# Attention and MLP on one core: loads queued earlier, pair 0 on hardware queues, two more pairs turned by transposing transfers

## The chip, the cores and the metric

One core of a Trainium2 chip. The metric is the device time of one execution in microseconds, median over several runs; lower is better. Engines are named as in the profile: PE (TensorE), PEld (its weight loads), DVE (VectorE), ACT (ScalarE), POOL (GpSimd), SP (SyncE). A "pair" is two of the twelve heads of one batch entry; there are 48 pairs. "Turning" q, k or x is transposing it for PE, either by matmuls against an identity on PE, or by a transposing transfer on SP's hardware queue.

## The reference

```python
# q, k, v: (8, 12, 448, 64) float32; w_in: (768, 2048); w_out: (2048, 768)
scores = (q @ k.transpose(0, 1, 3, 2)) / np.sqrt(64)
attn = np.exp(scores - scores.max(-1, keepdims=True))
attn = attn / (attn.sum(-1, keepdims=True) + 1e-09)
x = (attn @ v).transpose(0, 2, 1, 3).reshape(3584, 768)
h = x @ w_in
out = np.maximum(0.01 * h, h) @ w_out          # (3584, 768) float32
```

## The kernel before

Pairs 0 to 5 (batch entry 0) open the kernel: scores on PE, exponentials on ACT, weighted values on PE. From pair 6 on, "clusters" of attention work are woven between the matmuls of the MLP over the batch entry before. Loads of the first 18 pairs and of all weights go through POOL's software queue, which casts to bf16 on the way; they stand in POOL's program between casts that POOL does itself.

```python
def load_soft(u, n, which):            # n pairs of q, k or v in one transfer (POOL's queue)
    ...
def supply(u):                         # POOL's work in opening pair u
    if u == 0:
        cast(0, (2,), fast); cast(2, (0, 1), fast); cast(1, (2,), fast)   # fast: on DVE
        cast(3); cast(2, (2,))                                            # on POOL
        load(6)
        return
    load_w({1: 1}.get(u, 0))           # one of eight weight slices
    cast(u + 3)
    load({3: 8, 5: 10}.get(u, NU))     # two pairs
    load_w({2: 1, 4: 1, 5: 1}.get(u, 0))

def cluster(g):                        # t, r = divmod(g, 4); u = 3 * t
    if turn_q < NPE:                   # NPE = 14: pairs below it are turned on PE
        transposes(turn_q)
    ...                                # scores, exponentials, values
    if r < 3:
        cast(u + 3 + r)
        load(u + 5 + r)
        load_w({9: 1, 10: 1, 13: 1}.get(g, 0))   # the last three w_out slices
    if r > 0:
        dma_transposes(u + 2 + r)      # from pair NPE on: transposing transfer on SP

def mlp(i):
    ...                                # h = leaky(x @ w_in), 16 groups, then per output half w:
    for m in range(MD):                # MD = 16; m >= 8 with w = 1 reads the LAST w_out slice
        nc.tensor.matmul(ps[:, :NW], h[:, m, ts(c, P)], w_out_sb[:, m, ts(w, NW)], ...)
```

The softmax here doesn't subtract the row's maximum and nothing guards it: scores larger than these inputs give would overflow.

## Time and profile before

| | before |
|---|---|
| time, median | 421.32 us (421.07 to 422.21) |
| span in the profile | 418.9 us, granted clock 0.996 |
| PE busy | 407.3 us |
| first matmuls of the MLP start | 27.92 us |
| last w_out slice issued, landed | 59.41, 72.8 us |

PE is busy for 97% of the span, so time can be won only where PE waits, where it is slowed, or where it is given less work. The lines and their reading are in the prediction.

### The profile page before, as it was taken

The numbers are of one execution on the slowest core, as the hardware profiler recorded it, in microseconds if no ns is written. First come the engines' busy times: TensorE is split into PE (matmuls) and PEld (weight loads), VectorE is DVE, ScalarE is ACT, GpSimd is POOL, SyncE is SP. The second block draws the span as 40 slices with busy tenths as digits, with TensorE's granted clock in tenths as the row PEclk, the third lists the DMA queues.
The fourth block names the chain that finished last, engine by engine and source line by source line (L and its number), as shares of the span: only waits on it lengthen the run. The fifth ranks groups of instructions, "written<-read, shape, count | busy, mean of one in ns | idle before, by whom it ended". The sixth has DMA issues, their size and how long they took to land.

```text
span 418.9 us, 8949 instructions
## 1 busy us (share of the span) xinstructions
PE 407.3 (97%) x3730; PEld 235.4 (56%) x3744; DVE 104.0 (25%) x293; ACT 228.0 (54%) x321; POOL 107.3 (26%) x179
## 2 busy tenths in 40 slices
PE   7899999999999999999999999999999999999995
PEld 2565665554555566554556656554465666654562
DVE  3653342311223113220132212221022211310021
ACT  4897882467442784466724584467643587214200
POOL 8865765321111313120311212131130200000000
PEclk9899999999999999999999999999999999999999
DMA  8999999982666848585465847768264541130032
GB/s 103 191 203 174 160 195 159 192 217 71 161 162 174 180 113 196 140 210 119 110 160 155 214 112 176 196 150 187 77 170 127 127 49 24 50 88 0 0 77 76
DMA packets 96249, 57.00 MB, mean 136 GB/s; under 512 B 53200, under 2 KB 92624, under 8 KB 96208
## 3 DMA queue, kind: packets, MB, share of 16 engines
q1 hardware_dynamic: 76352, 43.94, 44.2%
q0 software_dynamic: 19856, 12.49, 22.0%
q8 instruction: 29, 0.48, 0.5%
q14 instruction: 12, 0.10, 0.1%
HBM read 45.61 MB, written 11.01 MB: 135 GB/s over the span
## 4 chain that ended last, share of the span: by engine, by line
PE 81%; DMA 12%; POOL 4%; issue 1%; DVE 0%; POOLq 0%
PE mm L330 33%; PE mm L301 31%; PE pv L245 10%; PE sc L224 8%; DMA fv<-in_v_dram 7%; DMA w_out_sb<-in_moe_w_out_dram 3%; DMA fk<-in_k_dram 2%; POOL fq L102 1%; POOL fk L102 1%; POOL v L137 1%; POOL qkb L135 0%; DVE o L334 0%; POOL fv L102 0%; PE tr L209 0%; POOL ident masks.py:199 0%
## 5 line engine op out<-in xcount | busy, mean ns | idle before, releaser
L233 ACT ACTIVATE e<-sc 112x896 bf16<-112x896 f32 x192 | 165.0, 915 | 105.4 <-PE sc L224 105.0
L330 PE MATMUL mm<-w_out_sb,h 128*128 128x384 bf16 x896 | 150.4, 326 | 0.6 <-DVE x L253 0.2
L301 PE MATMUL mm<-xT,w_in_sb 128*128 128x384 bf16 (+1 forms) x742 | 147.8, 352 | 0.9 <-DVE x L253 0.2
L330 PEld LDWEIGHTS <-h 128*128 128x128 bf16 x896 | 85.9, 98 | 55.7 <-issue 0.8
L301 PEld LDWEIGHTS <-w_in_sb 128*128 128x128 bf16 x768 | 72.9, 98 | 66.2 <-issue 1.2
L316 ACT ACTIVATE h<-mm 128x512 bf16<-128x512 f32 (+1 forms) x126 | 68.7, 546 | 58.6 <-PE mm L301 57.4
L245 PEld LDWEIGHTS <-e 112*128 112x128 bf16 x1536 | 56.9, 98 | 26.2 <-issue 16.5
L137 POOL CAST v<-fv 112x512 bf16<-112x512 f32 x30 | 18.6, 618 | 193.2 <-PE pv L245 189.3
L245 PE MATMUL pv<-v,e 112*128 112x65 bf16 x1536 | 65.4, 195 | 0.4 <-DVE v L137 0.4
L334 DVE COPY o<-mm 128x384 f32<-128x384 f32 x56 | 31.2, 558 | 134.0 <-PE mm L330 134.0
L252 DVE RECIPROCAL rec<-pv 112x4 f32<-112x4 f32 x96 | 17.5, 182 | 150.4 <-PE pv L245 149.8
L224 PE MATMUL sc<-qkT 64*128 64x448 bf16 x384 | 49.6, 357 | 0.9 <-DVE qkT L213 0.7
L253 DVE TENSOR_TENSOR x<-pv,rec 112x256 bf16<-112x256 f32 x96 | 40.8, 425 | 3.3
L224 PEld LDWEIGHTS <-qkT 64*128 64x128 bf16 x384 | 13.6, 94 | 18.4 <-issue 9.2
L135 POOL CAST qkb<-fq 112x512 bf16<-112x512 f32 x30 | 18.5, 616 | 2.5 <-POOL v L137 1.3
L135 POOL CAST qkb<-fk 112x512 bf16<-112x512 f32 x30 | 18.5, 616 | 0.5 <-DMA fk<-in_k_dram 0.3
L135 POOL COPY qkb<-fq 112x512 bf16<-112x512 bf16 x15 | 9.4, 626 | 15.2 <-DMA fq<-in_q_dram 14.5
L137 POOL COPY v<-fv 112x512 bf16<-112x512 bf16 x16 | 9.8, 618 | 9.5 <-DMA fv<-in_v_dram 5.8
L213 DVE COPY qkT<-tr 128x896 bf16<-128x896 bf16 (+1 forms) x15 | 8.8, 589 | 11.7 <-PE tr L209 11.7
L209 PE MATMUL tr<-ident,qkb 112*128 112x112 bf16 x112 | 8.8, 220 | 1.5 <-DVE qkb L135 1.3
L135 POOL COPY qkb<-fk 112x512 bf16<-112x512 bf16 x15 | 9.4, 626 | 2.2 <-DMA fk<-in_k_dram 1.9
L209 PEld LDWEIGHTS <-qkb 112*128 112x128 bf16 x112 | 7.0, 101 | 4.2 <-DVE qkb L135 2.7
(26 smaller groups left out, 51.9 us busy)
## 6 DMA issues: line engine op xcount, KB each, us to landing
fq<-in_q_dram SPq DMA_DIRECT2D x30, 224.0 KB, 3.2
fk<-in_k_dram SPq DMA_DIRECT2D x30, 224.0 KB, 3.3
fv<-in_v_dram SPq DMA_DIRECT2D x30, 224.0 KB, 3.8
w_in_sb<-in_moe_w_in_dram POOLq DMA_DIRECT2D x4, 768.0 KB, 11.9
w_out_sb<-in_moe_w_out_dram POOLq DMA_DIRECT2D x4, 768.0 KB, 10.9
out_dram<-o SPq DMA_DIRECT2D x8, 336.0 KB, 3.5
out_dram<-o SPq DMA_DIRECT2D x8, 288.0 KB, 2.7
fv<-in_v_dram POOLq DMA_DIRECT2D x9, 224.0 KB, 8.1
```

The lines of the kernel that those rows point to most:

```text
L135: by(qk_sb[u][:, x].rearrange("p so h d -> p h so d"), f)
L137: by(v_sb[u % NV][:, :, :, :D], f)
L209: nc.tensor.transpose(tr[:, i, ts(so, SC)], qk_sb[u][:, i, so], ident[:SC, :SC])
L224: nc.tensor.matmul(ps[:, j, :S], t[j * D:(j + 1) * D, S + c * SC:S + c * SC + P], t[j * D:(j + 1) * D, :S], start=True, stop=True,)
L233: nc.scalar.activation(e[:, :, c, :], sc_t.pop((u, c))[:SC, :, :S], AX.Exp, scale=scale)
L245: nc.tensor.matmul(ps[:, qc, :], e[:, at:at + P], vt[:, j, c, :], start=(c == 0), stop=(c == NSC - 1),)
L252: nc.vector.reciprocal(rec, ps[:SC, :, D:])
L253: nc.vector.tensor_mul(x_t[u][:, :, j, :], ps[:SC, :, :D], rec.to_broadcast([SC, NSC, D]))
L301: nc.tensor.matmul(open_t[m][:, :n], w_in_sb[:, kk, ts(m, P)], xT[:, kk, at:at + n], start=(fresh and kk == kks[0]), stop=(kk == KD - 1),)
L316: nc.scalar.activation(h[:, m, :n], open_t.pop(m)[:, :n], AX.Prelu, alpha=0.01)
L330: nc.tensor.matmul(ps[:, :NW], h[:, m, ts(c, P)], w_out_sb[:, m, ts(w, NW)], start=(m == 0), stop=(m == MD - 1),)
L334: nc.vector.tensor_copy(o[c][:, ts(w, NW)], ps[:, :NW])
```

## The change

The intent: loads enter the software queue earlier, so that POOL never blocks the next load with a cast whose data is still coming; pair 0 arrives sooner by hardware queues; ACT has three chunks of pair 0 in hand before PE turns pair 1; and PE is relieved of turning pairs 12 and 13. The core of it, cuts marked:

```diff
-    load_soft(0, 1, (0, 1))
+    load_one(0, 1, nc.sync)            # k of pair 0 on SP's queue
+    load_soft(0, 1, (0,))
 ...
     load_soft(1, 1, (0, 1))
-    load_soft(0, 2, (2,))
-    load(2)
-    load(4)
+    load_soft(2, 2, (0, 1))            # q, k of pairs 2, 3
+    load_soft(1, 2, (2,))              # v of pairs 1, 2
+    load_soft(4, 2, (0, 1))
+    load_soft(3, 2, (2,))
+    load_soft(5, 1, (2,))
     load_w(1)
 ...
+    nc.scalar.copy(gate[:, :1], gate[:, 1:])
+    load_one(0, 2, nc.scalar)          # v of pair 0 on ACT's queue
 ...
-    cast(0, (0, 1), fast)
+    cast(0, (1,), lambda o, i: (nc.scalar.copy(o[:, 0], i[:, 0]), fast(o[:, 1], i[:, 1])))
+    cast(0, (0,), fast)
+    cast(0, (2,), nc.scalar.copy)
 ...
-    NPE = 14
+    NPE = 12
 ...
+        for what, n in {0: [('qk', 2), ('v', 1), ('v', 2), ('load', 6)],
+                        1: [('qk', 3), ('qk', 4), ('v', 3), ('w', 1)],
+                        2: [('qk', 5), ('v', 4), ('v', 5), ('load', 8)], ...   # supply(u)
 ...
-            warm_up(4)
+            warm_up(2)
         expo(u, 1)
+        if u == 0:
+            scores(u, 2)               # ahead of transposes(1)
```

More of the change, by code (lines that the diff above doesn't have):

```diff
@@ L108, in load_soft, with load_one, load @@
                 raw.setdefault(u + i, {})[x] = half(t, i)
-    def load(u, queues=(nc.sync,) * 3):
+    def load_one(u, x, queue):
+        b, hp = divmod(u, HP)
+        t = ld_pool.tile([SC, 2, NSC, D], F32, name="f" + "qkv"[x])
+        queue.dma_start(
+            out=t.rearrange("p h so d -> p h (so d)"),
+            in_=(q, k, v)[x][b, 2 * hp:2 * hp + 2].rearrange("h (p so) d -> p h (so d)", so=NSC),
+        )
+        raw.setdefault(u, {})[x] = t
+    def load(u):
         if u >= NU:
@@ L116, in load @@
             return
-        b, hp = divmod(u, HP)
-        raw[u] = {}
-        for a, name, eng in zip((q, k, v), ("fq", "fk", "fv"), queues):
-            t = ld_pool.tile([SC, 2, NSC, D], F32, name=name)
-            eng.dma_start(
-                out=t.rearrange("p h so d -> p h (so d)"),
-                in_=a[b, 2 * hp:2 * hp + 2].rearrange("h (p so) d -> p h (so d)", so=NSC),
-            )
-            raw[u][len(raw[u])] = t
+        for x in range(3):
+            load_one(u, x, nc.sync)
     def cast(u, parts=(0, 1, 2), by=nc.gpsimd.tensor_copy):
@@ L131, in cast @@
             f = raw[u].pop(x)
-            if x == 0:
+            if u not in qk_sb:
                 qk_sb[u] = cast_pool.tile([SC, 2, NSC, 2, D], BF16, name="qkb")
@@ L162 @@
     nc.vector.memset(warm, 0.0)
+    gate = const_pool.tile([P, 2], F32)
+    nc.vector.memset(gate, 0.0)
+    nc.scalar.copy(gate[:, :1], gate[:, 1:])
+    load_one(0, 2, nc.scalar)
     def warm_up(n):
@@ L204, in transposes @@
             return
-        for parts in ((0,), (1,)) if u == 0 else ((0, 1),):
+        for parts in ((1,), (0,)) if u == 0 else ((0, 1),):
             tr = turn_tile(bank)
@@ L340, in supply @@
     def supply(u):
-        if u == 0:
-            cast(0, (2,), fast)
-            cast(2, (0, 1), fast)
-            cast(1, (2,), fast)
-            cast(3)
-            cast(2, (2,))
-            load(6)
-            return
-        load_w({1: 1}.get(u, 0))
-        cast(u + 3)
-        load({3: 8, 5: 10}.get(u, NU))
-        load_w({2: 1, 4: 1, 5: 1}.get(u, 0))
+        for what, n in {0: [('qk', 2), ('v', 1), ('v', 2), ('load', 6)], 1: [('qk', 3), ('qk', 4), ('v', 3), ('w', 1)], 2: [('qk', 5), ('v', 4), ('v', 5), ('load', 8)], 3: [('qk', 6), ('v', 6), ('w', 1)], 4: [('qk', 7), ('v', 7), ('w', 1)], 5: [('qk', 8), ('v', 8), ('load', 10), ('w', 1)]}[u]:
+            if what == "qk":
+                cast(n, (0, 1), fast if n in (2, 3) else nc.gpsimd.tensor_copy)
+            elif what == "v":
+                cast(n, (2,))
+            elif what == "load":
+                load(n)
+            else:
+                load_w(n)
     def first(u):
@@ L369, in first @@
             supply(u)
-        scores(u, 2)
+        if u > 0:
+            scores(u, 2)
         scores(u, 3)
```

## The prediction

> **What bounds the kernel now.** I read the page's busy shares first, then busy time by stretch, then the order of time of ScalarE (ACT) and TensorE (PE), then the chain of work that ended last.
>
> ```profile
> PE 407.3 (97%) x3730; PEld 235.4 (56%) x3744; DVE 104.0 (25%) x293; ACT 228.0 (54%) x321; POOL 107.3 (26%) x179
> ```
>
> TensorE is busy for 407.3 of 418.9 us, so only 11.6 us are open idle time. The last matmul group in order of time ends at 413.8, so about 5.1 us of it is the closing eviction and store, which the change doesn't touch; 1.2 us is the wait before the first warm-up matmul; some 5 us lie between, nearly all in the first 38 us. Busy is not full speed, though, so I took the start apart by stretch (columns: PE, weight loads, DVE, ACT, POOL, granted clock, DMA share, GB/s).
>
> ```profile
> 5.00:9.40 4.40, 3.43 (x30) 1.48 (x28) 2.26 (x6) 2.39 (x3) 4.40 (x7) 1.00 1.20 147
> 9.40:12.80 3.40, 1.74 (x28) 1.20 (x25) 1.47 (x4) 2.68 (x4) 2.21 (x4) 0.97 1.35 175
> 12.80:16.20 3.40, 3.40 (x37) 1.69 (x35) 1.96 (x6) 2.44 (x3) 2.94 (x6) 0.53 1.43 198
> 16.20:30.00 13.80, 13.42 (x217) 8.81 (x214) 8.94 (x25) 12.54 (x17) 11.84 (x19) 1.00 1.28 200
> ```
>
> From 9.4 to 12.8 us PE is half idle, and in the next 3.4 us it runs at a clock of 0.53. From 16 to 29 us ACT is nearly full: the six opening pairs are paced by the 24 exponentials. ACT's order of time shows where that row of exponentials is broken:
>
> ```profile
> 6.89 5.19 ACT L233 ACTIVATE e<-sc 112x896 bf16<-112x896 f32 x6 [4.87 <-PE sc L224]
> 13.63 3.58 ACT L233 ACTIVATE e<-sc 112x896 bf16<-112x896 f32 x4 [1.55 <-PE sc L224]
> 17.59 11.52 ACT L233 ACTIVATE e<-sc 112x896 bf16<-112x896 f32 x14 [0.38 <-PE sc L224]
> ```
>
> First exponential at 6.89, last ends at 29.11; 14 in 11.52 us is 0.823 us each, so 24 without a break would take 19.8 us, and 2.4 us of the 22.2 are lost. PE's order of time names the 1.55 us gap: the scores that ACT waits for stand on PE behind the turning of pair 2, and that waits for k of pair 2:
>
> ```profile
> 12.54 0.55 PE L209 MATMUL tr<-ident,qkb 112*128 112x112 bf16 x4 [0.81 <-DVE qkb L135]
> 13.03 0.93 PE L224 MATMUL sc<-qkT 64*128 64x448 bf16 x4
> ```
>
> The 0.93 beside the usual 0.55 is the cold clock. Lastly the chain: until 72.85 us it runs through transfers and the casts of GpSimd (POOL), after that through PE matmuls to the end.
>
> ```profile
> 39.09 7.19 DMA fv<-in_v_dram
> ...
> 48.36 6.02 DMA fv<-in_v_dram
> ...
> 59.41 13.39 DMA w_out_sb<-in_moe_w_out_dram
> 72.85 1.46 PE mm L330 x8
> ```
>
> The last w_out slice lands at 72.8 and releases PE at once. The PE group there took 5.60 us against 5.36 for its neighbours, so PE itself was only 0.24 us ahead of that transfer. Two paths are equally long at this point; to win, both must shorten.
>
> **What the Trainium skill says.**
> 1. "DMA: Bandwidth & Descriptors", section "Issuing engines are not separate DMA queues": transfers from SP, ACT and GpSimd share the same 16 engines; a second issuer saves only issue time. So moving k and v of pair 0 takes GpSimd's issue (0.66 us for k, in POOL's order of time) off the line, and no bytes. The trace fits: from 10 to 36 us the engines move about 200 GB/s whoever waits.
> 2. The same page, "Latency and other measured facts", gives a first byte of about 0.6 us for hardware and 1 us for software queues. The trace has no transfer on an idle hardware queue; the shortest landing of k is 2.9 us. I use 2.9 to 3.3 for both kinds.
> 3. "TensorE: Matmul & The Clock Gate", "What's actually happening": after an idle window of about 3.4 us the array runs at half clock until it has had a busy one. The trace agrees: 1.74 busy of 3.40 us, then a clock of 0.53 for 3.4 us.
> 4. "ScalarE: Activation LUTs", "What ACT_TABLE_LOAD costs": an ACTIVATE with immediates takes 186 ns plus 0.833 ns per element, the table load about 1.28 us. The trace has the load at 0.74 to 2.02, and 128x512 at 546 ns on average over two shapes.
>
> **The change part by part.** Instruction orders of the built programs confirm the moves; one table load remains.
>
> (a) *Start of pair 0.* Before: q landed at 4.31, k at 5.19 (DVE's waits), then 1.29 us to the first scores (6.48) and 0.41 to the first exponential (6.89). After: k goes out on SP at about 0.9, an estimate, lands at about 3.9, is cast half on DVE, half on ACT, and is turned while q is cast; q lands at 4.3 as before. q is now last: 4.3 + 0.1 + 1.3 = 5.7 to 5.9 for the first scores, 6.1 to 6.3 for the exponential. But ACT has v's cast ahead of the first exponential. v is issued after table load and gate copy, at about 2.3; landing takes 3 to 3.8 beside the queue, so 5.3 to 6.1; the cast of 512 elements is 0.6 us: 5.9 to 6.7. I choose 6.4 for the first exponential: **0.5 us gained**.
>
> (b) *The broken row.* k of pair 2 was cast at 12.19, the tenth transfer piece. Now q and k of pair 2 go out behind four small pieces and ahead of all v on that queue: one 0.70 us issue and the 0.66 us of k0 less in front, and one 1.2 us piece of transfer (landings at 9.86, 11.01, 12.19, 13.42 are 1.2 apart). I expect k of pair 2 at about 10.5, ready at 10.8. The seventh exponential falls due at 6.4 + 6 x 0.86 = 11.6; turning and scores need 0.5 + 0.4 us after 10.8, so 11.7. The 1.55 us gap goes to about 0.2, unless the clock falls again; the 0.38 gap probably stays or halves. **1.3 us gained**. "Pair 1 behind three chunks" gives ACT a third chunk in hand and shifts work on an idle PE, alone worth nothing, as pair 1 was turned in time before. Two warm-up matmuls less (0.26 us each) lie in idle time.
>
> (c) *Casts behind transfers.* POOL stood in front of unfinished transfers 4.39, 1.15 and 2.54 us (at 34.3, 37.1, 46.4) before it could issue the next; the queue ran dry and the rate fell to some 70 GB/s around 39 and 120 around 49. Now the loads of pairs 8 and 10 are ahead of weight slices: pair 8 issued about 20 instead of 25.3, pair 10 about 32 instead of 37.7. PE's own stall on the late k of pair 8 (transposes at 35.47 and 36.03 instead of together) ends: **0.3 us gained**. The two holes at 200 GB/s are worth about 1.3 + 0.8 us, with smaller ones perhaps 3: the last w_out slice should land near 70 instead of 72.85.
>
> (d) *Limit 14 to 12.* Pairs 12 and 13 leave PE for the hardware transposing transfer. On PE each cost 0.49 us (59.23 to 59.72, 67.02 to 67.51): **1.0 us gained**, all on the path. DVE loses 2 x 0.62 us, hidden. Two more transposing transfers of up to 8.9 us to landing: pair 12 has from its cast (54) to its scores (67), so it is hidden, but they share engines with w_out.
>
> PE would thus be at the last w_out slice at 72.6 - 0.5 - 1.3 - 0.3 - 1.0 = 69.5, and the slice arrives at about 70, or 70.5 with two more transposes ahead. From there on PE is busy throughout (339.9 of 346.05 us, the rest mainly the tail), nothing else changes, so the end moves by 72.85 - 70.2 or so: between 2.3 and 3.3. I take **2.8 us**: 421.3 - 2.8 = 418.5.
>
> **The rivals.**
> *The last w_out slice becomes the bound.* The chain speaks for it: it already is, by 0.24 us. Against it: issue waits only on POOL's order, and pair 8's values were used up by 53.4, so the issue can move from 59.4 to 56. If it moves by only 1 us: 420.3.
> *The cold clock stays or grows.* PE still waits for ACT between 8 and 10 us, with two warm-ups less. Half clock for 3.4 us makes PE, with about 3 us of work per pair, slower than ACT's 3.4 per pair, and costs up to 1.5 us: 419.5 to 420.
> *v's cast on ACT delays the first exponential.* If v lands at 7, nothing is gained at the start: 419.
> *All goes well.* An unbroken row (2.4), start at 6.2, w_out early: 4 to 4.5 us, 417.
>
> **Range and chances.** The sum of the good terms gives 416.9, that of one or two failing 420; runs of one kernel spread by about 1 us. So 416.8 to 420.3. Two per cent are 8.4 us, more than all the idle time outside the tail plus the two turns: faster 0.02. For slower by 8.4 us there is no mechanism: 0.01.
>
> **What would show each step.** (a) First exponential at 6.4 in ACT's order of time, not 6.9. (b) No gap over 0.5 us in the first 24 exponentials, and the last of them ending near 26.8 instead of 29.1. (c) No rate hole at 38 to 50 us, the last w_out slice landed by 70.5. (d) No PE transposes for pairs 12 and 13, no PE wait in their place. From 73 us on, both kernels show the same intervals at a constant offset. The prediction is wrong if the clock is at half for longer than before, or if PE waits over 1 us for a transfer between 25 and 73 us.

## The result, and the profile after

424.80 us median (423.67 to 425.09, four runs), against 421.35 for the kernel before in the same rounds. Ratio 1.0073, 95% interval 1.0050 to 1.0097: slower by 0.7%, where 0.7% faster was forecast. (Ratios are the mean time of one kernel's fast runs over that of the other's of the same rounds, so not quite the ratio of the medians.)

ACT's order of time in the opening, to set beside the three lines of before (start, length, engine, line, what; in brackets the idle time ahead of it and what ended it):

```profile
1.20 0.39 ACTq L113 DMA_DIRECT2D fv<-in_v_dram  x1
...
6.93 4.95 ACT L246 ACTIVATE e<-sc 112x896 bf16<-112x896 f32 x6 [2.13 <-PE sc L237]
12.90 3.59 ACT L246 ACTIVATE e<-sc 112x896 bf16<-112x896 f32 x4 [1.01 <-PE sc L237]
16.80 11.52 ACT L246 ACTIVATE e<-sc 112x896 bf16<-112x896 f32 x14 [0.32 <-PE sc L237]
```

The row of 24 exponentials starts where it did and ends at 28.3 instead of 29.1: the gap shrank from 1.55 to 1.01 us only. So PE leads by 0.8 us at the first MLP matmuls (27.14 against 27.92).

PE's order of time where the second half of the MLP begins. Before:

```profile
68.71 5.60 PE L330 MATMUL mm<-w_out_sb,h 128*128 128x384 bf16 x32
74.24 0.74 PE L224 MATMUL sc<-qkT 64*128 64x448 bf16 x6
82.44 5.34 PE L301 MATMUL mm<-xT,w_in_sb 128*128 128x512 bf16 x23
```

After:

```profile
66.37 4.06 PE L343 MATMUL mm<-w_out_sb,h 128*128 128x384 bf16 x24
75.00 2.72 PE L343 MATMUL mm<-w_out_sb,h 128*128 128x384 bf16 x8 [4.57 <-DMA w_out_sb<-in_moe_w_out_dram]
77.65 1.30 PE L237 MATMUL sc<-qkT 64*128 64x448 bf16 x6
...
86.87 3.40 PE L314 MATMUL mm<-xT,w_in_sb 128*128 128x512 bf16 x15
```

Here is the whole loss. PE arrives 2.3 us ahead of before (66.37 against 68.71), does 24 of 32 matmuls, and waits 4.57 us for the last w_out slice. Then eight matmuls take 2.72 us; before, the same eight took 1.46. The scores behind them take 1.30 instead of 0.74. Busy time by stretch gives the reason (columns as in the prediction):

```profile
70.00:74.00 4.00, 0.43 (x3) 0.14 (x2) 0.00 (x0) 0.00 (x0) 3.13 (x5) 0.90 1.32 153
74.00:78.00 4.00, 3.00 (x11) 1.14 (x12) 0.24 (x1) 0.00 (x0) 1.99 (x5) 0.50 1.41 174
```

The idle wait took PE to half clock (0.50). From the slice's landing to the first MLP group of the next batch entry it takes 86.87 - 75.00 = 11.87 us, before 82.44 - 72.85 = 9.59. So at that point the sum is: arrival 72.61 to 70.43, -2.18; wait 0.24 to 4.57, +4.33; half clock +2.28; together +4.43. The spans of the two profiles differ by 4.2 us, the medians by 3.5.

The chain of waits shows the slice, as it did before:

```profile
57.45 17.51 DMA w_out_sb<-in_moe_w_out_dram
75.00 2.72 PE mm L343 x8
```

It was issued 2 us earlier than before and took 17.5 us to land instead of 13.4. The transfers between 50 and 74 us suggest why (queue q0 is POOL's software queue, q1 the hardware queue of SP; packets, MB, share of 16 engines). Before:

```profile
q0 software_dynamic: 5682, 3.63, 115.6%
q1 hardware_dynamic: 1864, 0.45, 23.2%
```

After:

```profile
q0 software_dynamic: 4620, 3.09, 97.0%
q1 hardware_dynamic: 3447, 0.85, 40.6%
```

The hardware queue, almost all transposing transfers here, moved 0.40 MB more in 1583 more packets of some 250 bytes; the software queue moved 0.54 MB less in as many microseconds. And between 66 and 70 us of the changed kernel:

```profile
q0 software_dynamic: 558, 0.40, 104.2%
q1 hardware_dynamic: 558, 0.13, 56.3%
```

Packet for packet, one each in this stretch: one of some 250 bytes for one of some 700 (0.40 MB in 558).

### The profile page after: what moved, and what is told of

Its sections match the earlier page's. It is cut to its first block, busy times and chain, and to the rows that moved or that the text cites. A ratio compares the mean times of both kernels' runs of the same rounds, so it can differ in the third digit from the quotient of the medians.

```text
span 423.1 us, 8937 instructions
## 1 busy us (share of the span) xinstructions
PE 408.6 (97%) x3726; PEld 235.1 (56%) x3726; DVE 103.2 (24%) x292; ACT 228.9 (54%) x324; POOL 105.0 (25%) x177
## 4 chain that ended last, share of the span: by engine, by line
PE 87%; DMA 8%; POOL 2%; DVE 1%; issue 1%; POOLq 0%
PE mm L343 33%; PE mm L314 32%; PE pv L258 12%; PE sc L237 9%; DMA w_out_sb<-in_moe_w_out_dram 4%; DMA fv<-in_v_dram 2%; DMA fk<-in_k_dram 2%; PE tr L222 1%; POOL fq L102 1%; PE tr L279 1%; PE sc L314 1%; DVE x L266 1%; POOL fk L102 0%; POOL v L139 0%; DVE o L347 0%
## 5 line engine op out<-in xcount | busy, mean ns | idle before, releaser
L314 PE MATMUL mm<-xT,w_in_sb 128*128 128x512 bf16 (+1 forms) x756 | 148.6, 353 | 0.2 <-DVE x L266 0.2
L258 PEld LDWEIGHTS <-e 112*128 112x128 bf16 x1536 | 57.3, 98 | 26.7 <-issue 16.2
L265 DVE RECIPROCAL rec<-pv 112x4 f32<-112x4 f32 x96 | 17.5, 182 | 152.5 <-PE pv L258 151.8
L237 PEld LDWEIGHTS <-qkT 64*128 64x128 bf16 x384 | 13.8, 95 | 18.9 <-issue 10.5
L226 DVE COPY qkT<-tr 128x896 bf16<-128x896 bf16 (+1 forms) x13 | 7.6, 585 | 8.6 <-PE tr L222 8.5
L222 PE MATMUL tr<-ident,qkb 112*128 112x112 bf16 x96 | 7.6, 219 | 1.3 <-DVE qkb L137 1.3
L222 PEld LDWEIGHTS <-qkb 112*128 112x128 bf16 x96 | 6.0, 100 | 3.3 <-DVE qkb L137 1.8
```

The lines of the kernel that those rows point to most:

```text
L222: nc.tensor.transpose(tr[:, i, ts(so, SC)], qk_sb[u][:, i, so], ident[:SC, :SC])
L237: nc.tensor.matmul(ps[:, j, :S], t[j * D:(j + 1) * D, S + c * SC:S + c * SC + P], t[j * D:(j + 1) * D, :S], start=True, stop=True,)
L258: nc.tensor.matmul(ps[:, qc, :], e[:, at:at + P], vt[:, j, c, :], start=(c == 0), stop=(c == NSC - 1),)
L265: nc.vector.reciprocal(rec, ps[:SC, :, D:])
L314: nc.tensor.matmul(open_t[m][:, :n], w_in_sb[:, kk, ts(m, P)], xT[:, kk, at:at + n], start=(fresh and kk == kks[0]), stop=(kk == KD - 1),)
```

## The experiments

Theory: the two added transposing transfers alone slow the software queue, the slice lands late, PE waits, and the half clock follows. Rivals: the new order of loads makes it late; the transfers are late as a whole; the clock costs nothing. In each edit, "changed" is the changed kernel and "before" the one before it. The kernel before was timed beside each group of runs: 421.36 us (E1 to E4), 421.99 (E5 to E8) and 420.53 (E9 to E11).

### E1: the limit back at 14

```diff
 changed:
-    NPE = 12
+    NPE = 14
```

> The changed kernel with the limit set back to 14: pairs 12 and 13 are turned on TensorE again. Theory (the two added transposing transfers halve the rate of the software queue, so that the last w_out slice lands late): with them gone the slice, issued near 57.5 us, lands about 13.4 us later as before, near 71; PE needs it at about 71.4, so the 4.6 us wait and the half clock after it vanish; about 420.0 us against 421.35. Rival (the new order of loads itself makes the slice late): the slice still lands near 74 to 75 and the time stays at 423 or more.

418.57 us (417.66 to 419.10), ratio 0.9928 (0.9903 to 0.9953). The slice landed by PE's arrival: there is no wait for it, and the group takes its usual time, as PE's order of time shows.

```profile
67.38 5.36 PE L343 MATMUL mm<-w_out_sb,h 128*128 128x384 bf16 x32
72.68 0.74 PE L237 MATMUL sc<-qkT 64*128 64x448 bf16 x6
73.35 0.69 PE L258 MATMUL pv<-v,e 112*128 112x65 bf16 x16
```

It was issued at 55.41 and took 13.9 us to land (columns: queue, transfers, size of one, us to landing):

```profile
w_out_sb<-in_moe_w_out_dram POOLq DMA_DIRECT2D x1, 768.0 KB, 13.9
```

So everything in the change except this one number, taken together, makes the kernel faster; undoing the number is worth 6 us. The rival of the load order falls.

### E2: the kernel before with the limit at 12

```diff
 before:
-    NPE = 14
+    NPE = 12
```

> The kernel before with only the limit changed from 14 to 12. Theory: the last w_out slice, which there landed at 72.8 us with 0.24 us of PE wait, lands 3 to 4 us later beside two more transposing transfers, PE arrives 1 us earlier, waits 4 to 5 us and then runs 3 us at half clock; about 425 us. Rival (transposes are free, the load order is to blame): 1.0 us of PE work gone, 420.4 us.

426.49 us (425.02 to 428.16), ratio 1.0124 (1.0088 to 1.0159). This is the converse: the number alone makes the old kernel slower. PE's waits name the same place, and the slice, issued at the same time as before (59.46 and 59.41), took 17.8 us to land instead of 13.4:

```profile
PE mm L330 <- DMA w_out_sb<-in_moe_w_out_dram: 4.7, 1, 4.7
```

This run also shows that the old opening varies: its gap behind the sixth exponential was 2.77 us, against 1.55 in the profile of before.

### E3: the last w_out slice issued three clusters earlier

```diff
 changed:
-            load_w({9: 1, 10: 1, 13: 1}.get(g, 0))
+            load_w({9: 1, 10: 2}.get(g, 0))
```

> The changed kernel with the last w_out slice issued three clusters earlier, directly behind the third (near 49 us instead of 57.5). Theory (everything the change costs comes from that one late slice): the slice lands by 66, PE doesn't wait, and the 2.35 us by which PE led at 66 us carry to the end, with the 0.24 us wait of the kernel before gone too: 418.8 us. Rival (the transfers are late as a whole, so that the wait moves to the loads of pairs 14 and 15 pushed behind the slice): a new wait of PE for scores or DVE of pair 14 between 70 and 85 us, and 421 us or more.

421.51 us, and very uneven: 418.76, 420.70, 422.32, 424.04. The median is the rival's, and a wait appeared in the stretch that it named; but the fastest run is as fast as the theory said, so the four runs do not decide alike. The profile is of the slowest of the four. PE no longer waits for w_out, but for x, turned by a transposing transfer:

```profile
PE mm L314 <- DMA xT<-x: 5.2, 1, 5.2
```

Its chain of waits shows how (start, length, what):

```profile
54.69 18.57 DMA fv<-in_v_dram
...
75.49 9.66 DMA xT<-x
85.16 0.04 issue
85.20 4.97 PE mm L314 x13
```

The loads of pairs 14 and 15, now behind two w_out slices, took up to 18.6 us. POOL cast them late, SP's queue turned pair 14 late, and the transfer that turns x stood behind that on the same queue. So in this run the new order only chose who is late; that the 16 engines carried too much in this stretch is argued, not shown.

### E4: PE kept busy in the wait

```diff
 changed, in mlp():
             for m in range(MD):
+                if i == 0 and c == 0 and w == 1 and m == MD // 2:
+                    dummy = ps_g.tile([P, 4 * P], F32, name="mm", tag="g")
+                    for _ in range(20):
+                        nc.tensor.matmul(dummy, warm[:, :P], warm, start=True, stop=True)
```

> The changed kernel with 20 idle matmuls of 128x512 (4.3 us at full clock) put into PE's order just ahead of the matmul that waits for the last w_out slice. The wait stays as long, but PE is busy in it. Theory (of the loss, some 2.3 us are the half clock that follows the idle wait): no half clock after 75 us, 422.5 us. Rival (the clock costs nothing, only the wait does): 424.8 us, or a little more.

422.09 us (421.65 to 422.22), 2.7 us less than the changed kernel's 424.80 of the earlier group. The slice still took 17.2 us, but the eight matmuls behind it take their usual time:

```profile
69.60 4.48 PE L346 MATMUL mm<-warm 128*128 128x512 bf16 x19
74.72 1.46 PE L347 MATMUL mm<-w_out_sb,h 128*128 128x384 bf16 x8 [0.64 <-DMA w_out_sb<-in_moe_w_out_dram]
```

Twenty useless matmuls made the kernel faster (19 of them are in the records), by 2.7 of the 6.2 us between the changed kernel and E1. Most of that is the half clock: from the slice's landing to the next batch entry's MLP it takes 84.32 - 74.72 = 9.60 us, against 11.87, so 2.27 us less. Another 0.28 us is a slice that landed earlier.

### E5: pairs 2 and 3 loaded one by one

```diff
 changed with NPE = 14 (E1):
-    load_soft(2, 2, (0, 1))
+    load_soft(2, 1, (0, 1))
+    load_soft(3, 1, (0, 1))
```

> On the changed kernel with the limit at 14 (418.6 us in the first call): q and k of pairs 2 and 3 in two transfers of one pair each instead of one of both. Theory (the opening row of exponentials is set by the arrival of k of pair 2, cast at 11.7 us there): k of pair 2 is cast near 9.5 to 10, the 0.94 us gap behind the sixth exponential shrinks below 0.4 us, the 24th exponential ends near 27.2 instead of 28.2, and the time falls by 0.6 to 1.0 us, to about 417.8. Rival (two more issues of 0.7 us on POOL, or v of pair 1 behind them, take the place): a new gap behind the tenth exponential, 418.6 us or more.

418.42 us (418.18 to 419.50), the same as E1. k of pair 2 was cast at 10.1 us instead of 11.7, but in the profiled run, the slowest of the four, PE fell to half clock in the opening and its own work became the bound:

```profile
9.40:12.80 3.40, 3.17 (x32) 1.82 (x32) 1.65 (x6) 2.94 (x4) 2.15 (x4) 0.50 1.21 150
```

A gap of 0.86 us stayed in ACT's row. Inconclusive from this profile, so E9 repeats it together with E8.

### E6: pair 0 back on the software queue

```diff
 changed with NPE = 14 (E1):
-    load_one(0, 1, nc.sync)
-    load_soft(0, 1, (0,))
+    load_soft(0, 1, (0, 1))
 ...
     load_soft(1, 1, (0, 1))
+    load_soft(0, 1, (2,))
 ...
-    load_one(0, 2, nc.scalar)
 ...                                   # k cast on DVE, v on POOL, q turned first
```

> On the changed kernel with the limit at 14: k and v of pair 0 back on the software queue (k behind q, v behind k of pair 1), cast on DVE and POOL; the rest of the new order stays. Theory (the hardware queues save two issues of about 0.7 us ahead of pair 2): q of pair 0 lands near 4.3 instead of 5.3, the first exponential stays near 6.9, k of pair 2 is cast near 12.2 instead of 11.7; 419.1 us against 418.6. Rival (the same bytes over the same engines: the queue doesn't matter): 418.6 us.

419.82 us (419.25 to 420.69), ratio 0.9950 beside 0.9917 for E8 in the same group. The hardware queues are worth something, in the direction forecast: 1.3 us by the medians, with intervals that overlap. The profile explains little of it: q of pair 0 was cast at 4.36 us instead of 5.27, k of pair 2 at 11.91 instead of 11.72, the row of exponentials ended at 28.32 instead of 28.16. The rest of the size stays open.

### E7: the limit at 13

```diff
 changed:
-    NPE = 12
+    NPE = 13
```

> The changed kernel with the limit at 13: one pair, not two, leaves TensorE for a transposing transfer. Theory (each such transfer delays the last w_out slice by about 2 us; it landed at 75.0 with two, and with none at or before 71.4, when PE wanted it): slice near 72, PE at 71 to 71.4, a wait of 0 to 1.5 us and no half clock: 418 to 419.5 us. Rival (the two transfers hurt only together, by holding the SP queue): 0.5 us of PE work gone and no wait, 418.1 us; rival (any one is enough): 424 us.

420.66 us (418.04 to 420.94; one run of four near the forecast, three above it). PE waited, but the half clock did not follow (the granted clock is 1.00 from 70 to 78 us):

```profile
PE mm L343 <- DMA w_out_sb<-in_moe_w_out_dram: 2.0, 1, 2.0
```

The slice took 15.2 us from issue to landing. With no transfer of this kind added it took 11.9 to 14.1 us (six profiles: before, E1, E5, E6, E8, E9), with two 17.2 to 17.8 (E4, the changed kernel, E2). It was also issued late here, at 58.07, against 55.4 to 57.3 in the profiles of the new order with the limit at 14. That is not the added transfer's doing: POOL had waited for v of a pair until 53.41, and the transfer went out at 58.89 only. So by the medians one transfer costs more than the 0.5 us that it takes off PE, and the landing is graded, which neither rival allows; how much of this run's 2.0 us wait comes from the transfer and how much from the late issue stays open.

### E8: v of pair 0 issued late

```diff
 changed with NPE = 14 (E1):
-    load_one(0, 2, nc.scalar)          # behind the gate copy
 ...
-    cast(0, (2,), nc.scalar.copy)
+    load_one(0, 2, nc.scalar)          # behind ACT's half of the cast of k; v cast on POOL
```

> On the changed kernel with the limit at 14: v of pair 0 goes out on the ACT queue only behind ACT's half of the cast of k, so behind k's landing at 3.6 us instead of at 1.2, and is cast on POOL. Theory (v ran ahead of q on the engines and cost q 1 us, but the row of exponentials is set by k of pair 2, so that nothing is won): q of pair 0 lands near 4.4 to 4.6 instead of 5.3, the first exponential starts near 6.2 instead of 6.9, and the gap behind the sixth grows by as much; 418.6 us. Rival (the first exponential sets the end): 0.6 us faster, 418.0 us.

418.54 us (418.30 to 418.68), as E1. q of pair 0 was cast at 4.65 instead of 5.27, the first exponential started at 6.63 instead of 6.88:

```profile
6.63 4.95 ACT L245 ACTIVATE e<-sc 112x896 bf16<-112x896 f32 x6 [2.82 <-PE sc L236]
12.12 3.34 ACT L245 ACTIVATE e<-sc 112x896 bf16<-112x896 f32 x4 [0.54 <-PE sc L236]
```

The gap behind the sixth exponential was smaller too, 0.54, not larger as forecast, because k of pair 2 came at 11.06. That may be more than chance: from 5 to 9.4 us the DMA engines moved 175 GB/s here and 190 in E9, the two runs with v issued late, against 120 to 146 in the changed kernel, E1, E4 to E7, E10 and E11. Why is not shown. The end of the gap follows that cast by 1.0 to 1.4 us in each of these kernels (before 12.19 and 13.63, changed 11.47 and 12.90, E8 11.06 and 12.12), which supports that k of pair 2, not the first exponential, sets the row (in E5, at half clock, and E9 something else came last). The time shows no gain above its spread.

### E9: E8 and E5 together

> The two earlier edits together on the changed kernel with the limit at 14: v of pair 0 issued late, and q and k of pairs 2 and 3 split by pair. In the run with the split alone k of pair 2 was cast at 10.1 us, but PE happened to run at half clock from 8 to 15 us and hid it. Theory (with k of pair 2 early and PE warm the row of 24 exponentials has no gap over 0.3 us): the last of the 24 ends near 26.8 us against 27.5 with v late alone, 417.8 us. Rival (PE's work in the opening, or its clock, is the next bound): a gap of 0.5 us or more stays, 418.5 us.

419.22 us (418.58 to 420.15), ratio 0.9961: a gap over 0.5 us stayed, as the rival said, though by another wait than it named. k of pair 2 was cast at 9.33 us, and now v of pair 0 was late: its cast stands on POOL behind the two added issues and starts 1.2 us later than in E8 (10.78 against 9.57).

```profile
PE pv L258 <- POOL v L139: 1.7, 1, 1.7
```

The gap in the row grew to 1.42 us, and the clock fell to 0.51 from 12.8 to 16.2 us behind it. In these profiles of the opening, what one arrival gains the next takes.

### E10 and E11: useless copies, small packets and large

```diff
 changed with NPE = 14 (E1):
+    spare = const_pool.tile([SC, 2, 8, 128 + 16], BF16)      # E11: [SC, 2, 1, 1024 + 16]
     def dma_transposes(u):
+        if 12 <= u < 14:
+            nc.sync.dma_start(out=spare[:, u - 12, :, :128],     # E11: :1024
+                in_=qk_sb[u].rearrange("p i so h d -> p (i so h d)").rearrange("p (r n) -> p r n", r=8))
```

> The changed kernel with the limit at 14, so with pairs 12 and 13 turned on TensorE, plus two useless copies of their cast q and k to a spare tile, SBUF to SBUF, on the SP queue at the places of the two transposing transfers: the same 229 KB each, cut into runs of 256 bytes (896 each). Theory (the hardware queue takes turns with the software queue packet by packet, and small packets are what costs): as late a last w_out slice as with the transposes, some 17 us behind its issue instead of 13.9, a PE wait of 1 to 4 us, 420.5 to 424 us. Rivals: it is the bytes (then this run and the one with long runs cost the same), or it is the transposing itself (then both stay at 418.6).

> As the run with copies in runs of 256 bytes, but in runs of 2048 bytes (112 for each copy), the same bytes. Theory (packets count, not bytes): an eighth of the packets, so the last w_out slice lands within 0.7 us of 13.9 us behind its issue, no PE wait, 418.6 to 419 us. Rival (bytes count): as slow as the other, 420.5 us or more.

E10, runs of 256 bytes: 421.18 us (420.25 to 423.24; the profile is of the fastest); the slice took 16.5 us.

```profile
w_out_sb<-in_moe_w_out_dram POOLq DMA_DIRECT2D x1, 768.0 KB, 16.5
PE mm L350 <- DMA w_out_sb<-in_moe_w_out_dram: 1.4, 1, 1.4
```

E11, the same bytes in runs of 2048: 419.11 us (418.88 to 419.21); 14.2 us, no wait.

```profile
w_out_sb<-in_moe_w_out_dram POOLq DMA_DIRECT2D x1, 768.0 KB, 14.2
```

The two queues from 50 to 74 us, E10:

```profile
q0 software_dynamic: 4728, 3.14, 94.4%
q1 hardware_dynamic: 3673, 0.91, 42.4%
```

E11:

```profile
q0 software_dynamic: 5424, 3.48, 105.5%
q1 hardware_dynamic: 2144, 0.92, 30.1%
```

Equal bytes on the hardware queue, 1529 packets fewer, and the software queue moves 0.34 MB more. So most of the lateness comes without any transposing, and the bytes alone do not make it: with the same bytes, many small packets cost the slice 2.3 us more than few large ones, and the kernel 2.1 us by the medians. They do not account for all of it. With true transposes the slice took some 1 us longer still, and the changed kernel is 6.2 us slower than E1, though it has 1.0 us less work on PE; the rest is not settled. The Trainium skill states a mechanism in "DMA: Bandwidth & Descriptors", section "Queues, rings and completion order": each engine goes round the queues that have work "at *packet* granularity". The case agrees as to the turns, with 558 packets against 558 above, though the page counts several descriptors to a packet, and no run shows that the profile's packets are the same thing. Nor do the two runs tell whether a small packet costs by its turn or by the time for which it holds an engine.

## Why the prediction was wrong

**The step that failed** is in parts (c) and (d), the landing of the last w_out slice: "or 70.5 with two more transposes ahead". Two transposing transfers were given 0.5 us; the slice landed at 75.0. The other half of the step, "near 70 instead of 72.85", held without the transfers: 69.3 in E1, 68.4 to 70.3 in E5, E6, E8 and E9. From issue to landing the slice took 17.5 us with them and 13.9 without (E1). Its issue, too, came later than in E1 (57.45 against 55.41), but not because of them as far as the runs show: E2 and the kernel before differ in the limit alone and issue it at 59.46 and 59.41. The text knew that "they share engines with w_out", but did not work the 0.5 us out: twice 229 KB at its own 200 GB/s is 2.3 us, an estimate, and small packets cost more than their bytes (E10 against E11). So PE waited 4.57 us, which is also one of the signs of being wrong that the prediction named, a wait of PE of over 1 us for a transfer. A pair turned on PE cost 0.5 us; turned by transfer in this stretch it cost 2 to 3 us of the median (E7 and the changed kernel against E1, which ran in other groups).

**The second failed step** is that a wait costs its own length. The rivals name the last slice as a possible bound, and give the half clock only to the opening. The wait of 4.6 us brought the half clock with it, 2.3 us more (E4). So did waits of 4.72 us in E2 and 5.17 us in E3; waits of 2.0 us in E7 and 1.4 us in E10 did not. The section that the prediction quotes for the opening ("TensorE: Matmul & The Clock Gate", "What's actually happening": half clock after an idle window of about 3.4 us) fits here. In the opening itself the trace shows no such window: PE was busy for 1.74 of the 3.40 us ahead of the half clock.

**Part (a)**, 0.5 us from an earlier first exponential: it started at 6.93, no earlier. v of pair 0 was issued at 1.20, not at 2.3. The copy meant as a gate did not hold it: the table load still ran until 2.02 and the copy itself only at 2.03. "Perfetto Trace Analysis", section "Sequencer Loop", says why: the sequencer pushes engine instructions into a queue, where they wait, and reads the next. The trace agrees: the transfer was issued 0.8 us before the table load ended. So v and k went over the engines ahead of q, which came at 5.33 instead of 4.31. Putting v behind a real wait (E8) brought q back to 4.65, but bought no time that shows above the spread. This suggests, and does not show, that gain (a) was not on the path beside (b), so that the two could not be added.

**Part (b)**, 1.3 us from k of pair 2: cast at 11.47, not 10.5, so the gap was 1.01, not 0.2. From 6 to 12 us the software queue moved 113 to 149 GB/s, from 12 us on about 190. Before, the step up came at 8 us. What holds it back there is not settled (see E8 for what goes with it). The clock fell here as before, to 0.84 from 9.4 to 12.8 us and 0.66 in the next 3.4 us; in the profiles of E1, E4, E6, E7, E8 and E10 it stayed at 1.00, in those of E5, E9 and E11 it fell to about 0.5. So small differences between single profiles of the opening are not to be trusted.

That ACT has three chunks in hand ahead of the turning of pair 1 was not tried alone.

**Part (c)**: the PE stall on k of pair 8 went as forecast (its eight transposes run in one piece at 34.70), about 0.35 us. Issues moved earlier, by the 5 us expected for pair 10 (32.61 against 37.68). The hole in the rate at 38 to 40 us closed (197 GB/s, before 71), that at 48 to 50 us hardly did (134, before 119).

**Part (d)**: the PE work went as forecast, 0.5 us for each pair. **The offset from 73 us on** was constant, as forecast, but with the other sign.

The size that was forecast for the whole, 418.5 us, is what E1 gives (418.57), but by another sum, since there no pair leaves PE; that they agree is luck. E1, E5, E6, E8, E9 and E11, all with the limit at 14, beat both kernels (ratios to the one before of 0.991 to 0.996).

## What to carry to other kernels

Before moving work from PE to transfers, look at what else the DMA engines carry in that stretch, and count packets as well as bytes: here, from 66 to 70 us, a queue of packets of some 250 bytes took turns one for one with a queue of some 700. Where two paths meet with a slack of 0.24 us, moving work from one to the other needs the length of both after the move. And price an idle wait on PE with the half clock that may follow it: in the MLP of these runs it did behind waits of 4.57 us and more, and did not behind waits of 2.0 us and less.

## What the Trainium skill lacked or had wrong

- "DMA: Bandwidth & Descriptors" states the turns by packet but not what they do to a queue of large loads: here a weight slice took 11.9 to 14.1 us to land with no transposing transfer added (six profiles), 15.2 with one of 229 KB, 17.2 to 17.8 with two, 16.5 with two plain copies in 256-byte runs, and 14.2 with the same bytes in 2048-byte runs.
- The same page, section "DMA Transpose (X-bar)", gives no time to landing beside other traffic: in the changed kernel a transposing transfer of q and k took 8.1 to 12.3 us between 50 and 72 us.
- No page read for this case accounts for the low rate of the software queue early in this program: 113 to 149 GB/s from 6 to 12 us and about 190 after that in the changed kernel.
- "TensorE: Matmul & The Clock Gate" agrees with the runs on the half clock after a long wait (4.57 us); it lacks the remedy of useless matmuls put into the wait, measured here: 20 of them took the time from 424.80 to 422.09 us.
